# First batch of an attention and squared-ReLU kernel: another order of key scores, value sums and loads, zero products between the scores, and a shorter lag of the first output blocks

## The chip, the cores and the metric

The kernel runs on one core of a Trainium2 chip. The metric is the device time of one execution in microseconds (us), lower is better. TensorE is called PE, its weight loads PEld, VectorE DVE, ScalarE ACT, GpSimd POOL, and the queue that issues the transfers SP, as in the profile.

## The reference

Four batches of 12,480 tokens with 128 channels go through an attention with 49 agents, and the result through a two-layer network with 2,048 hidden units:

```python
def sm(a, b):
    s = (a @ b.transpose(0, 2, 1)) / np.sqrt(128)
    s = s - s.max(-1, keepdims=True)
    e = np.exp(s)
    return e / (e.sum(-1, keepdims=True) + 1e-09)
agent_v = sm(agents, k) @ v                  # 49 agents look at all keys of a batch
x = (sm(q, agents) @ agent_v).reshape(B * S, D)
h = x @ w_in                                 # 128 -> 2048
g = np.maximum(h, 0.0) ** 2
out = g @ w_out                              # 2048 -> 128
```

All of it is float32. The two weight matrices come as float64.

## The kernel before

*Pieces.* The 12,480 keys of a batch are cut into 13 pieces (`NS`) of 8 chunks (`G`) of 120 keys (`CH`). Queries are cut in the same way into groups of 960 tokens, 52 groups over the four batches. For a group the network runs in 16 blocks (`NF`) of 128 hidden units, so there are 832 blocks, counted by `i`.

*A block.* `mm1(i)` (L480) multiplies the group's attention weights, kept as a high and a low part, by `W`, the product of the batch's agent values and `w_in` (made by `w_make`, L356, L369, L371). `relu` (L484) and `square` (L488) run on ACT, `high` (L492) and `low` (L496) on DVE split the result in two parts, and `mm2` (L508) adds the block's product with `w_out` (as `wo_hi` and `wo_lo`) into two PSUM banks per group, in two halves of six matmuls. Between the halves of an `mm2` each bank changes the half of the rows that feeds it; an empty instruction on POOL's queue (`pass_on`, L161) takes the first half's end, and the second half waits for it (`take_over`). `mm2` of block i - `LAG` stands at place i, with `LAG` 6.

*The first batch.* Before any block can run, `W` of the first batch must be there, and for that all of its keys and values. Stage by stage: 12 products of zeros (`warm_up`, L652, 128x128 by 128x512, bf16); for each of 13 pieces a load, `k_scores` (L179: 8 float32 matmuls of a 128x120 key chunk as weights with the 49 agents, 16 records on PE), `k_copy` on ACT (L218) and `k_pmax` on DVE (L221); the maximum over pieces (`k_max`, steps 0 to 5, on DVE and PE). The maximum is taken twice: over the first 6 pieces (`S1`, into `mMs`), so that their exponentials can be taken early, and over all 13 (`mM`); `p_scale` corrects the sums of the first six. `k_sub` (L248) and `k_exp` (L251) follow per piece, then `v_acc_whole` (L298: 8 matmuls with 129 columns, 16 records) adds the piece's value sum into one of the two PSUM banks `vps` (pieces 0 to 5 into the first, 6 to 12 into the second). All 13 value sums come after all 13 key scores and the scores of the first query group (`q_scores`). Then `a_first` and `w_make` make `W`.

*Conversion.* `w_in` and `w_out` come in four pieces each as raw bits (`raw_load`). `to_f32` makes float32 of a piece in six steps, five on DVE (L85 to L90) and one on ACT (L86). `wo_split` makes `wo_hi` on ACT (L111) and `wo_lo` on POOL (L113). The last piece of `w_out` is converted during the first blocks.

*Order.* Nothing is left to a scheduler: `at(t, f, ...)` notes a step with a time, and the steps are issued in the order of these times; each engine works through its own list in this order and waits at semaphores. Steps of the first stage have times from `Z` = -100 on, the blocks have the time i. Extra work between the blocks (scores of later groups and of the next batch, `q_half`, `k_pair`) is placed by a planner (`chain`, with the sets `taken` and `banks`) or by hand for the first few: the pairs of key scores of batch 1 stand at 4.5 and 6.5.

*Buffers.* Loads of keys, values and queries rotate through 6 buffers (`io`), raw pieces through the 5 buffers that later hold `low` results (tag "gl"). SP issues loads in the order of the list `loads`, and waits with each until its buffer is free.

Of the kernel before, what the change touches and what calls it, by code (L numbers as in the profile page):

```python
# [17 lines left out]
P = 128  # L18
# [7 lines left out]
def agent_attention_relu2_kernel(ctx: ExitStack, tc: tile.TileContext, qT, kT, v, agT, w_in, w_out, outT):  # L26
# [10 lines left out]
    NF = F // P  # L37
    NS = NCH // G
# [29 lines left out]
    PW = 512  # L68
# [2 lines left out]

    raws = {}

    def raw_load(t, src):
        raws[t, src is wi_bits] = raw = ew.tile([P, PW, 2], U32, name="raw", tag="gl", bufs=5)
        nc.sync.dma_start(out=raw, in_=src[:, t * PW:(t + 1) * PW, :])

    def to_f32(raw, dst):

        lo, hi = raw[:, :, 0], raw[:, :, 1]  # L80
        p = ew.tile([P, PW], U32, name="cv_p", tag="g", bufs=3)
        x = ew.tile([P, PW], F32, name="cv_x", tag="gh", bufs=5)
        ts, stt = nc.vector.tensor_scalar, nc.vector.scalar_tensor_tensor
        return [
            lambda: ts(out=p, in0=hi, scalar1=20, scalar2=0x7FF, op0=ALU.logical_shift_right, op1=ALU.bitwise_and),  # L85
            lambda: nc.scalar.activation(p, p, AF.Relu, bias=ebias, scale=float(1 << 23)),  # L86
            lambda: ts(out=x.bitcast(U32), in0=hi, scalar1=0xFFFFF, scalar2=0x100000, op0=ALU.bitwise_and, op1=ALU.bitwise_or),
            lambda: stt(out=x, in0=lo, scalar=2.0 ** -32, in1=x.bitcast(U32), op0=ALU.mult, op1=ALU.add),
            lambda: stt(out=p, in0=hi, scalar=0x80000000, in1=p, op0=ALU.bitwise_and, op1=ALU.bitwise_or),
            lambda: stt(out=dst, in0=x, scalar=2.0 ** -20, in1=p.bitcast(F32), op0=ALU.mult, op1=ALU.mult),  # L90
        ]

    cv, wo = {}, {}
# [5 lines left out]

    def wo_make(t, step):  # L100
        if step == 0:
            wo[t] = ew.tile([P, PW], F32, name="wo_f", tag="gh", bufs=5)
            cv["o"] = to_f32(raws.pop((t, False)), wo[t])
        cv["o"][step]()

    def wo_split(t, step):
# [186 lines left out]
    S1 = 6  # L293
# [254 lines left out]
    def chain(t, todo):  # L548

        first = prev = None
        while todo:
            n = 1
            while todo[0][0] == "PE" and n < len(todo) and (todo[n][1] in reads_bank and todo[n][0] != "PE" or todo[n][1:-1] == todo[n - 1][1:-1] and todo[n][1] is not k_max):
                n += 1
            t += hop[prev][todo[0][0]] if prev else 0
            while True:
                g, p, ts = t, None, []
                for e, f, *_ in todo[:n]:  # L560
# [42 lines left out]
    def plan_turns(s):  # L603
        _, end = chain(max(ends[s] + 2, (s - 1) * NF), [("PE", q_transpose, s), ("ACT", q_copy, s)])
        at(end + .9, q_spread, s)
        assert end + 3 < s * NF, (s, end)
# [49 lines left out]
        early.close()  # L656
        ps_a[0] = ctx.enter_context(tc.tile_pool(name="ps_a", bufs=1, space=bass.MemoryType.PSUM))

    Z, KT, KP, VP = -100.0, 6.3, 1.7, 1.87
    FULL = (0, 1, 2, 3, 4, 5)  # L660
    loads = [(k_load, 0, n) for n in range(NS)]
    for x, *load in ((3, raw_load, 0, wi_bits), (6, raw_load, 1, wi_bits), (9, raw_load, 2, wi_bits), (13, raw_load, 3, wi_bits), (16, raw_load, 0, wo_bits)):
        loads.insert(x, load)
    loads += [(q_load, 0), *((v_load, 0, n) for n in range(NS)), (q_load, 1), *((k_load, 1, n) for n in range(AHEAD))]
    for x, t in ((22, 1), (26, 2), (30, 3)):
        loads.insert(x, (raw_load, t, wo_bits))
# [4 lines left out]
    def convert(f, n, times):  # L671
        for x, t in enumerate(times):
            at(Z + t, f, n, x)

    tk = [KT + KP * n + (.9 if n > S1 else 0) for n in range(NS + 1)]
    for n in range(NS):
        at(Z + tk[n], k_scores, 0, n)
        at(Z + tk[n] + KP + .01, k_copy, n)
        at(Z + tk[n] + KP + .05, k_pmax, n)
    for n in range(3):  # L680
        t = tk[n * 3 + (1 if n else 0)] + KP
        convert(win_make, n, (t + .6, t + .61, t + 1, t + KP + .7, t + KP + 1.3, t + 2 * KP + .7))
    t1, t2 = tk[S1], tk[NS] + 1.7
    for x, t in zip((0, 2, 3, 4, 5), (t1 + .7, t1 + 1.85, t1 + 2.3, t1 + KP + 2.3, t1 + KP + 2.8)):
        at(Z + t, k_max, x, S1, m2s[:, 0:1], mMs)
    for x, t in zip(FULL, (tk[NS] - 1.3, tk[NS] + .7, t2, t2 + .6, t2 + 2.4, t2 + 2.9)):
        at(Z + t, k_max, x)
    tv = [t2 + .5 + VP * n + (.5 if n else 0) + (1 if n > S1 + 2 else 0) for n in range(NS + 1)]
    for n in range(NS):
        at(Z + tv[n], v_acc_whole, n, vps)  # L690
        t = t1 + KP + 3 + .9 * n if n < S1 else t2 + 4 + 1.3 * (n - S1)
        at(Z + t, k_sub, n, nc.vector, mMs if n < S1 else mM)
        at(Z + t + .55, k_exp, n)
    for x, t in ((0, t2 + 3), (1, t2 + 3.1), (2, tv[S1] + .2), (3, tv[NS])):
        at(Z + t, p_scale, x, vps)
    t = tk[NS]
    for f, y in ((q_scores, 0), (q_max, 1.75), (q_sub, 2.4), (q_exp, 3), (q_total, 5.2), (q_norm, 6), (q_hi, 6.6), (q_lo, 7.2)):
        at(Z + t + y, f, 0, *([nc.vector] if f in (q_norm, q_lo) else []))
    at(Z + tv[S1 + 3] - 1, q_transpose, 0)
    at(Z + tv[S1 + 3] + .1, q_copy, 0)  # L700
    at(Z + tv[S1 + 3] + .2, q_spread, 0)
    for n in range(4):
        t = t2 + 7 + 3.8 * n
        convert(*((win_make, 3) if n == 0 else (wo_make, n - 1)), (t, t + .01, t + .4, t + 1.3, t + 2, t + 2.7))
        if n:
            at(Z + t + 3.4, wo_split, n - 1, 0)
            at(Z + t + 3.5, wo_split, n - 1, 1)
    t = tv[NS]
# [6 lines left out]
    for f in range(1, F // 512):  # L715
        for x, y in ((0, -.5), (2, -.49), (3, .06)):
            at(f + y, w_make, 0, f, x)
    convert(wo_make, 3, [-Z + .5 + .4 * x for x in range(6)])
    for x in range(2):
        at(3.5 + .1 * x, wo_split, 3, x)  # L720
    at(2.9, begin)
    at(3.5, q_half, 1, 0)
    at(4.02, q_half, 1, 1)
    at(4.03, q_shift, 1)
    _, ends[1] = chain(4, [("ACT", q_exp, 1), ("DVE", q_total, 1), ("DVE", q_norm, 1, nc.vector), ("ACT", q_hi, 1), ("DVE", q_lo, 1, nc.vector)])
    plan_turns(1)
    at(3.55, k_load, 1, AHEAD)
    for n, t in ((0, 4.5), (2, 6.5)):
        for x in range(2):
            at(t + .6 * x, k_pair, 1, n, x)  # L730
        at(t + 1, kp_copy, n, 2)
        at(t + 1.05, kp_max, n, 2)
    banks.update(range(10))
    taken.update((e, t) for e in ("ACT", "DVE") for t in (3, 4, 5, 6, 7, 8))
    plan_queries_early(2, 9, False)
    for s in range(3, NSG):
        plan_queries(s)
# [7 lines left out]
        ready = plan_values(b, ready, b * NS * NF)  # L745

    for i in range(NG + LAG):
        j, late = i - LAG, i < LAG or (i - LAG) % NF == 0
        if i < NG:
            at(i if late else i + .01, mm1, i)  # L750
            at(i + .1, relu, i)
            at(i + 1.2, square, i)
            at(i + 1.35, high, i)
            at(i + 3.3, low, i)
        if j >= 0:
            at(i + (.01 if late else 0), mm2, j, 0)
# [31 lines left out]
```

## Time and profile before

| what | value |
|---|---|
| runs of the kernel | 1990.84 to 1992.5 us, median 1991.76 (3 runs) |
| profiled execution | 1987.69 us, span 1985.9 us |
| busy: PE, PEld | 1970.5 us (99%), 1902.2 us (96%) |
| busy: DVE, ACT, POOL | 1777.6 us (90%), 1748.1 us (88%), 119.4 us (6%) |
| granted TensorE clock, mean over the span | 0.989 |
| moved by DMA | 121.31 MB, 61 GB/s in the mean |

The span goes from the first to the last instruction of the profiled execution, and the execution's own time is 1.8 us longer; this execution was 4.1 us shorter than the median of the runs. "Granted clock" is the share of full speed at which TensorE was allowed to run. In the profile's views a line stands for one or more instructions of the same kind, with the tiles written and read (`out<-in`), their number, and times in us; a bracket or a "<-" names what ended an engine's idle time. Lines are those of the kernel listed above.

### The profile page before, as it was taken

What the parts mean: (1) busy time and instruction counts of PE and PEld (TensorE: products, weight loads), DVE (VectorE), ACT (ScalarE), POOL (GpSimd) and SP (SyncE); (2) the same over time, 40 slices, a digit from 0 to 9 for tenths busy, and PEclk for the clock granted to TensorE, in tenths of its full rate; (3) what the DMA queues carried; (4) which work ended last, traced back from release to release, by engine and by line L of the source; (5) the groups of instructions that cost most, each with busy time, mean ns of one, the idle gap of its engine ahead of it and who ended that gap; (6) DMA issues with size and microseconds to landing.
All of it is one profiled execution on the core that took longest, in us unless ns stands there. A gap on an engine that the chain in (4) does not pass through costs nothing.

```text
span 1985.9 us, 47810 instructions
## 1 busy us (share of the span) xinstructions
PE 1970.5 (99%) x19919; PEld 1902.2 (96%) x19920; DVE 1777.6 (90%) x2434; ACT 1748.1 (88%) x2118; POOL 119.4 (6%) x56
## 2 busy tenths in 40 slices
PE   9999999999999999999999999999999999999998
PEld 8799999999998999999999899999999999999997
DVE  4677999999989999999998999999998998989887
ACT  2577998998889898998998999999999999999997
POOL 0100010000000040110000030020000000000000
PEclk6899999999999999999999999999999999999999
DMA  8431122122102112112111111121110101010000
GB/s 290 139 108 56 36 81 95 66 70 96 35 29 76 57 59 86 56 49 97 46 39 56 35 53 64 40 76 36 56 39 29 45 25 49 25 48 25 33 21 21
DMA packets 37434, 121.31 MB, mean 61 GB/s; under 512 B 4216, under 2 KB 9696, under 8 KB 37216
## 3 DMA queue, kind: packets, MB, share of 16 engines
q1 hardware_dynamic: 37216, 118.25, 17.5%
q8 instruction: 156, 2.56, 0.5%
q14 instruction: 62, 0.51, 0.1%
HBM read 82.89 MB, written 25.56 MB: 55 GB/s over the span
## 4 chain that ended last, share of the span: by engine, by line
PE 96%; ACT 2%; DVE 1%; issue 1%; POOLq 0%; ACTq 0%
PE out L508 54%; PE h L480 27%; PE ps_att L190 7%; PE ps_att L449 2%; PE ps_att L278 2%; PE out L298 1%; PE h L179 1%; ACT r L484 1%; ACT g L488 1%; PE ps_one L179 1%; DVE gl L496 1%; PE ps_att L362 0%; DVE gh L492 0%; PE out L652 0%; ACT w_a L369 0%
## 5 line engine op out<-in xcount | busy, mean ns | idle before, releaser
L484 ACT ACTIVATE r<-h 128x960 f32<-128x960 f32 x832 | 811.8, 976 | 167.3 <-PE h L480 141.7
L496 DVE TENSOR_TENSOR gl<-g,gh 128x960 fp32r<-128x960 f32 x832 | 958.6, 1152 | 0.0
L488 ACT ACTIVATE g<-r 128x960 f32<-128x960 f32 x832 | 834.5, 1003 | 2.2 <-DVE gl L496 1.3
L508 PE MATMUL out<-gh,wo_hi 64*128 64x480 f32 x3328 | 823.0, 388 | 5.5 <-POOLq L161 3.4
L508 PE MATMUL out<-gh,wo_lo 64*128 64x480 f32 x3328 | 804.3, 377 | 0.0
L508 PE MATMUL out<-gl,wo_hi 64*128 64x480 f32 x3328 | 803.0, 377 | 0.0
L492 DVE CAST gh<-g 128x960 fp32r<-128x960 f32 x832 | 558.8, 672 | 152.5 <-ACT g L488 98.7
L508 PEld LDWEIGHTS out<-gh,wo_hi 64*128 64x128 f32 x3328 | 471.8, 184 | 21.4 <-POOLq L161 9.6
L508 PEld LDWEIGHTS out<-gh,wo_lo 64*128 64x128 f32 x3328 | 476.7, 186 | 7.6
L508 PEld LDWEIGHTS out<-gl,wo_hi 64*128 64x128 f32 x3328 | 474.4, 185 | 9.7
L480 PE MATMUL h<-p_a,w_a 49*128 49x480 f32 x1664 | 410.7, 388 | 1.7 <-ACT r L484 1.1
L480 PE MATMUL h<-p_a,w_b 49*128 49x480 f32 x1664 | 402.0, 377 | 0.0
L480 PE MATMUL h<-p_b,w_a 49*128 49x480 f32 x1664 | 401.1, 376 | 0.0
L480 PEld LDWEIGHTS h<-p_a,w_a 49*128 49x128 f32 x1664 | 236.0, 184 | 10.0 <-ACT r L484 2.9
L480 PEld LDWEIGHTS h<-p_a,w_b 49*128 49x128 f32 x1664 | 237.3, 185 | 7.6 <-DVE w_b L371 0.4
L480 PEld LDWEIGHTS h<-p_b,w_a 49*128 49x128 f32 x1664 | 238.6, 187 | 4.9
L248 POOL TENSOR_TENSOR sk<-sk,mM 120x392 f32<-120x392 f32 x39 | 111.5, 2859 | 1230.7 <-PE out L508 645.3
L190 PEld LDWEIGHTS ps_att<-ag_sb,qt 64*120 64x120 f32 x1632 | 114.4, 181 | 1.2
L190 PE MATMUL ps_att<-ag_sb,qt 64*120 64x49 f32 x1632 | 106.5, 257 | 0.0
L190 PEld LDWEIGHTS ps_att<-ag_sb,kt 64*120 64x120 f32 x1248 | 79.3, 189 | 2.7 <-issue 1.8
L190 PE MATMUL ps_att<-ag_sb,kt 64*120 64x49 f32 x1248 | 76.0, 268 | 1.7 <-issue 1.7
L449 PEld LDWEIGHTS ps_att<-ident_r,pp 64*113 64x113 f32 (+1 forms) x816 | 55.0, 175 | 1.0 <-DVE pm L212 0.3
(126 smaller groups left out, 997.5 us busy)
## 6 DMA issues: line engine op xcount, KB each, us to landing
vt<-v SPq DMA_DIRECT2D x52, 516.0 KB
kt<-kT SPq DMA_DIRECT2D x52, 480.0 KB
qt<-qT SPq DMA_DIRECT2D x52, 480.0 KB
outT<-ob SPq DMA_DIRECT2D x51, 480.0 KB
p_b<-p_a SPq DMA_DIRECT2D x104, 91.9 KB
raw<-w_in SPq DMA_DIRECT2D x4, 512.0 KB
raw<-w_out SPq DMA_DIRECT2D x4, 512.0 KB
outT<-ob SPq DMA_DIRECT2D x2, 240.0 KB
```

What stands on the lines that cost most here:

```text
L179: nc.tensor.matmul(ps[:CH, c * A:(c + 1) * A], kt[:, c, :], ag_sb[:, b, :], start=True, stop=True)
L190: mm = nc.tensor.matmul(ps[:CH, u, r * A:(r + 1) * A], cols[u][r][rows], ag_sb[rows, b, :], start=x == 0 and r == 0, stop=x == 1 and r == ...
L248: eng.tensor_tensor(out=piece(n), in0=piece(n), in1=m.rearrange("p (o a) -> p o a", o=1).to_broadcast([CH, G, A]), op=ALU.subtract)
L278: nc.tensor.matmul(ps[:A2, t, :VW], pe[rows, c, :], vs[rows, c], start=c == 0, stop=c == G - 1)
L298: nc.tensor.matmul(ps[x][:A, :C + 1], piece(n)[:, c, :], vt[:CH, c, :], start=n in (0, S1) and c == 0, stop=c == G - 1 and n in (S1 - 1, N ...
L449: nc.tensor.matmul(ps[:M, t, c * n:(c + 1) * n], pps[s % 2][rows, c, :], ident_r[rows, rows], start=True, stop=True)
L480: nc.tensor.matmul(hs[i][:, t, :TT], w, p, start=n == 0, stop=n == 2)
L484: nc.scalar.activation(rs_[i], hs.pop(i)[:, :, :TT], AF.Relu)
L488: nc.scalar.activation(gs[i], rs_.pop(i), AF.Square)
L492: nc.vector.tensor_copy(ghs[i], gs[i])
L496: nc.vector.tensor_tensor(out=gls[i], in0=gs.pop(i), in1=ghs[i].bitcast(F32), op=ALU.subtract)
L508: mm = nc.tensor.matmul(o[u][:, :TT], w[rows, j, :], g[rows, u, :], start=j == 0 and x == 0 and n == 0, stop=j == NF - 1 and x == 1 and n ...
```

## The change

Seven things are changed, all of them in the first batch's stage and the first 20 blocks:

1. TensorE's order is written as one queue. Key scores of pieces 0 to 8 come first, with products of zeros between them (one after pieces 0 and 1, two after pieces 2 to 8: 16 in all, into the second `vps` bank, which holds nothing yet). Then value sums 0 to 3 alternate with key scores 9 to 12; then the query scores, the last maximum's two products with value sum 4 between them, and value sums 5 to 12.
2. The loads stand in that order, values among the keys.
3. `k_sub` and `k_exp` stand ahead of the value sum that needs them.
4. The seven conversions that lie before the blocks get times of their own. The last piece of `w_out` is loaded into an `io` buffer, converted at places 7.6 to 10.1 (before 0.5 to 2.5) in other buffers, and split at 11.5 (before 3.5).
5. `mm2` lags four blocks up to place 7, five up to place 13, and six after; at places 7 and 13 (`SKIP`) there is no `mm2`, and a pair of key scores of batch 1 stands there in its place.
6. `low` stands at i + 2.32 up to block 7 (before i + 3.3).
7. The first score half of query group 1 goes to 3.08 (before 3.5), the second to 4.005 (before 4.02); the planner may place other scores only from place 15 on (before 10).

```diff
+    SKIP = (7, 13)
...
+    queue = []
+    for n in range(S1 + 3):
+        queue += [("k", n, 1.7), ("w", 1 if n < 2 else 2, .22 if n < 2 else .44)]
+        if n in (S1, S1 + 1):
+            queue.append(("s", 2 * (n - S1 + 1), .45))
+    for n in range(S1 + 3, NS):
+        queue += [("v", n - S1 - 3, 1.87), ("k", n, 1.7)]
+    queue += [("q", 0, 1.7), ("m", 2, .45), ("v", S1 - 2, 1.87), ("m", 4, .45)]
+    for n in range(S1 - 1, NS):
+        queue.append(("v", n, 1.87))
+        if n == S1 + 2:
+            queue.append(("t", 0, 1.0))
+    for what, n, d in queue:
+        order[what, n] = t
...
+        at(Z + t, f, *args)
+        t += d
...
-    loads = [(k_load, 0, n) for n in range(NS)]
+    loads = [(k_load, 0, n) for n in range(S1 + 3)]
+    for n in range(S1 + 3, NS):
+        loads += [(v_load, 0, n - S1 - 3), (k_load, 0, n)]
+    loads += [(q_load, 0), *((v_load, 0, n) for n in range(NS - S1 - 3, NS)), (q_load, 1), *((k_load, 1, n) for n in range(AHEAD))]
+    for x, t, src in ((2, 0, wi_bits), (5, 1, wi_bits), (8, 2, wi_bits), (13, 3, wi_bits), (16, 0, wo_bits), (23, 1, wo_bits), (27, 2, wo_bits), (37, 3, wo_bits)):
+        loads.insert(x, (raw_load, t, src, x > 35))
...
-        t = t1 + KP + 3 + .9 * n if n < S1 else t2 + 4 + 1.3 * (n - S1)
+        t = t1 if n == 0 else max(t1 + .6 * n, order["v", n - 1] - .5) if n < S1 else t2 if n == S1 else order["v", n - 2] + .6
         at(Z + t, k_sub, n, nc.vector, mMs if n < S1 else mM)
         at(Z + t + .55, k_exp, n)
...
-    convert(wo_make, 3, [-Z + .5 + .4 * x for x in range(6)])
+    convert(wo_make, 3, [-Z + 7.6 + .5 * x for x in range(6)])
     for x in range(2):
-        at(3.5 + .1 * x, wo_split, 3, x)
+        at(11.5 + .1 * x, wo_split, 3, x)
...
-    for n, t in ((0, 4.5), (2, 6.5)):
+    for n, t in ((0, SKIP[0]), (2, SKIP[1])):
         for x in range(2):
-            at(t + .6 * x, k_pair, 1, n, x)
+            at(t - .005 + .025 * x, k_pair, 1, n, x)
...
     for i in range(NG + LAG):
-        j, late = i - LAG, i < LAG or (i - LAG) % NF == 0
+        lag = LAG - sum(i <= x for x in SKIP)
+        j, late = i - lag, i < lag or i in SKIP or (i - lag) % NF == 0
+        if i in SKIP:
+            j = -1
         if i < NG:
...
-            at(i + 3.3, low, i)
+            at(i + (2.32 if i <= SKIP[0] else 3.3), low, i)
```

More of the change, by code (lines that the diff above doesn't have):

```diff
@@ L72, in agent_attention_relu2_kernel, with raw_load, to_f32 @@
     raws = {}
-    def raw_load(t, src):
-        raws[t, src is wi_bits] = raw = ew.tile([P, PW, 2], U32, name="raw", tag="gl", bufs=5)
+    def raw_load(t, src, late=False):
+        raws[t, src is wi_bits] = raw = (io if late else ew).tile([P, PW, 2], U32, name="raw", tag="io" if late else "gl", bufs=None if late else 5)
         nc.sync.dma_start(out=raw, in_=src[:, t * PW:(t + 1) * PW, :])
-    def to_f32(raw, dst):
+    def to_f32(raw, dst, late=False):
         lo, hi = raw[:, :, 0], raw[:, :, 1]
-        p = ew.tile([P, PW], U32, name="cv_p", tag="g", bufs=3)
-        x = ew.tile([P, PW], F32, name="cv_x", tag="gh", bufs=5)
+        pool, tags = (wk, ("pe", "pe")) if late else (ew, ("g", "gh"))
+        p = pool.tile([P, PW], U32, name="cv_p", tag=tags[0], bufs=3)
+        x = pool.tile([P, PW], F32, name="cv_x", tag=tags[1], bufs=3 if late else 5)
         ts, stt = nc.vector.tensor_scalar, nc.vector.scalar_tensor_tensor
@@ L101, in wo_make @@
         if step == 0:
-            wo[t] = ew.tile([P, PW], F32, name="wo_f", tag="gh", bufs=5)
-            cv["o"] = to_f32(raws.pop((t, False)), wo[t])
+            late = t > 2
+            wo[t] = (io if late else ew).tile([P, PW], F32, name="wo_f", tag="io" if late else "gh", bufs=None if late else 5)
+            cv["o"] = to_f32(raws.pop((t, False)), wo[t], late)
         cv["o"][step]()
@@ L657, in begin @@
         ps_a[0] = ctx.enter_context(tc.tile_pool(name="ps_a", bufs=1, space=bass.MemoryType.PSUM))
-    Z, KT, KP, VP = -100.0, 6.3, 1.7, 1.87
-    FULL = (0, 1, 2, 3, 4, 5)
-    loads = [(k_load, 0, n) for n in range(NS)]
[L662 to L666, printed above, removed]
+    Z = -100.0
+    order, t = {}, 6.3
+    queue = []
[12 more added lines that the diff above has]
+        order[what, n] = t
+        f, args = {"k": (k_scores, (0, n)), "w": (warm_up, (n, 1)), "s": (k_max, (n, S1, m2s[:, 0:1], mMs)), "m": (k_max, (n,)),
+                   "v": (v_acc_whole, (n, vps)), "q": (q_scores, (0,)), "t": (q_transpose, (0,))}[what]
+        at(Z + t, f, *args)
+        t += d
+    last = t
+    assert all(order["v", n] > order["k", n] for n in range(NS))
+    loads = [(k_load, 0, n) for n in range(S1 + 3)]
[4 more added lines that the diff above has]
+        loads.insert(x, (raw_load, t, src, x > 35))
     for n, (f, *args) in enumerate(loads):
@@ L673, in convert @@
             at(Z + t, f, n, x)
-    tk = [KT + KP * n + (.9 if n > S1 else 0) for n in range(NS + 1)]
     for n in range(NS):
[L677 to L684, printed above, removed]
+        t = order["k", n] + 1.7
@@ L685, in agent_attention_relu2_kernel @@
+        at(Z + t + .01, k_copy, n)
+        at(Z + t + .05, k_pmax, n)
+    for x, t in ((0, order["k", S1 - 1] + 2.4), (3, order["s", 2] + .45), (5, order["s", 4] + .45)):
         at(Z + t, k_max, x, S1, m2s[:, 0:1], mMs)
-    for x, t in zip(FULL, (tk[NS] - 1.3, tk[NS] + .7, t2, t2 + .6, t2 + 2.4, t2 + 2.9)):
+    for x, t in ((0, order["k", NS - 1] + .7), (1, order["k", NS - 1] + 2.4), (3, order["m", 2] + .45), (5, order["m", 4] + .45)):
         at(Z + t, k_max, x)
-    tv = [t2 + .5 + VP * n + (.5 if n else 0) + (1 if n > S1 + 2 else 0) for n in range(NS + 1)]
+    t1, t2 = order["s", 4] + .7, order["m", 4] + .7
@@ L689, in agent_attention_relu2_kernel @@
     for n in range(NS):
-        at(Z + tv[n], v_acc_whole, n, vps)
-        t = t1 + KP + 3 + .9 * n if n < S1 else t2 + 4 + 1.3 * (n - S1)
+        t = t1 if n == 0 else max(t1 + .6 * n, order["v", n - 1] - .5) if n < S1 else t2 if n == S1 else order["v", n - 2] + .6
         at(Z + t, k_sub, n, nc.vector, mMs if n < S1 else mM)
         at(Z + t + .55, k_exp, n)
-    for x, t in ((0, t2 + 3), (1, t2 + 3.1), (2, tv[S1] + .2), (3, tv[NS])):
+    for x, t in ((0, t2 + .6), (1, t2 + .7), (2, order["v", S1 + 1]), (3, last)):
@@ L695, in agent_attention_relu2_kernel @@
         at(Z + t, p_scale, x, vps)
-    t = tk[NS]
-    for f, y in ((q_scores, 0), (q_max, 1.75), (q_sub, 2.4), (q_exp, 3), (q_total, 5.2), (q_norm, 6), (q_hi, 6.6), (q_lo, 7.2)):
+    t = order["q", 0] + 1.7
+    for f, y in ((q_max, .05), (q_sub, .7), (q_exp, 1.2), (q_total, 5.2), (q_norm, 6), (q_hi, 6.6), (q_lo, 7.2)):
         at(Z + t + y, f, 0, *([nc.vector] if f in (q_norm, q_lo) else []))
-    at(Z + tv[S1 + 3] - 1, q_transpose, 0)
-    at(Z + tv[S1 + 3] + .1, q_copy, 0)
-    at(Z + tv[S1 + 3] + .2, q_spread, 0)
@@ L702, in agent_attention_relu2_kernel @@
[L702 to L708, printed above, removed]
+    t = order["t", 0] + 1
+    at(Z + t, q_copy, 0)
+    at(Z + t + .1, q_spread, 0)
+    gap = 3.6
+    for n in range(7):
+        t = (9, 15, 27, 31.2, 35, 46, 52)[n]
+        d = 1.6 if n < 2 else 1
+        convert(*((win_make, n) if n < 4 else (wo_make, n - 4)), (t, t + .01, t + .4, t + 1 * d, t + 2 * d, t + 3 * d))
+        if n > 3:
+            at(Z + t + 3.6, wo_split, n - 4, 0)
+            at(Z + t + 3.7, wo_split, n - 4, 1)
@@ L709, in agent_attention_relu2_kernel @@
+    t = last
     at(Z + t + .1, warm_up, 3, 0)
@@ L717, in agent_attention_relu2_kernel @@
             at(f + y, w_make, 0, f, x)
-    convert(wo_make, 3, [-Z + .5 + .4 * x for x in range(6)])
+    convert(wo_make, 3, [-Z + 7.6 + .5 * x for x in range(6)])
     for x in range(2):
-        at(3.5 + .1 * x, wo_split, 3, x)
[L721 to L724, printed above, removed]
+        at(11.5 + .1 * x, wo_split, 3, x)
+    at(3.07, begin)
+    at(3.08, q_half, 1, 0)
+    at(4.005, q_half, 1, 1)
+    at(4.04, q_shift, 1)
+    banks.update([*range(5), *(x + y for x in SKIP for y in range(3))])
     _, ends[1] = chain(4, [("ACT", q_exp, 1), ("DVE", q_total, 1), ("DVE", q_norm, 1, nc.vector), ("ACT", q_hi, 1), ("DVE", q_lo, 1, nc.vector)])
+    taken.update((e, t) for e in ("ACT", "DVE") for x in SKIP for t in (x, x + 1))
     plan_turns(1)
     at(3.55, k_load, 1, AHEAD)
-    for n, t in ((0, 4.5), (2, 6.5)):
+    for n, t in ((0, SKIP[0]), (2, SKIP[1])):
         for x in range(2):
-            at(t + .6 * x, k_pair, 1, n, x)
[L731 to L734, printed above, removed]
+            at(t - .005 + .025 * x, k_pair, 1, n, x)
+        at(t + .5, kp_copy, n, 2)
+        at(t + .55, kp_max, n, 2)
+    banks.update(range(SKIP[1] + 2))
     plan_queries_early(2, 9, False)
```

## The prediction

> **What bounds the kernel now.** I read the page first (busy shares, then the 40 slices), then the core cut into windows at the moments where the granted clock changes, then the chain that ended last, the waits of PE, and the groups of instructions by shape up to 130 us.
>
> ```profile
> PE 1970.5 (99%) x19919; PEld 1902.2 (96%) x19920; DVE 1777.6 (90%) x2434; ACT 1748.1 (88%) x2118; POOL 119.4 (6%) x56
> ...
> PEclk6899999999999999999999999999999999999999
> ```
>
> TensorE is busy 99% of the span, so only what shortens TensorE's own work, or raises its clock, can move the end. The clock is short of full in the first two slices alone, which is where the whole change lies. The windows show where (columns: span, then busy time and count of each engine, granted clock, DMA share, GB/s):
>
> ```profile
> 6.77:10.18 3.41, 3.41 (x35) 3.41 (x34) 1.04 (x3) 0.50 (x2) 0.00 (x0) 1.00 0.98 310
> 10.18:13.59 3.41, 3.41 (x35) 3.41 (x35) 2.59 (x6) 1.76 (x4) 0.00 (x0) 1.00 1.03 420
> 13.59:17.01 3.42, 3.38 (x33) 3.29 (x32) 2.26 (x5) 1.26 (x3) 0.00 (x0) 1.00 1.02 416
> 17.01:44.31 27.30, 27.30 (x137) 26.88 (x136) 15.11 (x30) 7.50 (x16) 0.00 (x0) 0.50 0.75 268
> 44.31:47.73 3.42, 3.42 (x17) 2.88 (x16) 0.27 (x3) 0.53 (x1) 0.00 (x0) 0.50 0.81 297
> 47.73:70.06 22.33, 22.33 (x209) 21.92 (x208) 18.03 (x35) 9.35 (x18) 4.85 (x3) 1.00 0.86 278
> ...
> 78.45:81.86 3.41, 2.89 (x19) 1.54 (x18) 2.24 (x4) 3.41 (x6) 0.00 (x0) 1.00 0.00 0
> 81.86:85.27 3.41, 2.54 (x40) 2.20 (x36) 3.41 (x6) 3.30 (x5) 0.39 (x1) 1.00 0.01 2
> 85.27:95.51 10.24, 8.85 (x76) 8.66 (x78) 6.01 (x12) 4.50 (x6) 1.35 (x1) 0.50 0.01 2
> 95.51:98.93 3.42, 3.31 (x20) 2.34 (x20) 2.43 (x3) 2.28 (x3) 0.00 (x0) 0.50 0.00 0
> ```
>
> The clock is halved twice: from 17.01 to 47.73 (30.72 us) and from 85.27 to 98.93 (13.66 us). Half of that, 15.4 and 6.8 us, is lost. The full stretch before the first fall is 10.24 us; 10.24, 30.72 and 13.66 are 3, 9 and 4 times 3.41, so the clock is judged every 3.41 us. In the three windows before the first fall PE is busy without a gap, so it is not idle time that lowers it. The chain (start, length, what) shows what the array streams there:
>
> ```profile
> 1.22 5.30 PE out L652 x12
> 6.52 1.80 PE h L179 x16
> ...
> 13.36 1.68 PE h L179 x16
> ...
> 33.55 3.20 PE ps_one L179 x16
> ...
> 46.95 0.56 PE ps_one L243 x2
> 47.52 14.42 PE out L298 x128
> 61.94 0.91 PE h L449 x10
> 62.85 7.22 PE out L298 x64
> ...
> 71.39 1.20 PE out L652 x5
> 72.59 1.09 PE ps_one L356 x2
> ...
> 113.25 0.66 PE out L508 x6
> ```
>
> A value-sum record takes 7.22/64 = 113 ns for 129 columns, 0.87 ns a column. A key-score record has 49 columns, worth 43 ns of streaming, and takes 1.68/16 = 105 ns: the weight load sets its time (PEld 3.41 of 3.41). So key scores stream 41% of the time, and value sums 100%. Under 41% the clock fell after three windows (the third, with a gap, has 39%). Before the second fall I add up, from the same rows, three w_make records and six pairs of block matmuls of 0.22 us (about 64%), then four such pairs and two score halves (about 40%). The clock rose after 44.31:47.73, which holds 2.6 us of value sums (about 82%).
>
> **The change, part by part.** All times are against the profiled execution, 1987.69 us with a span of 1985.9; the runs have a median of 1991.76, so I subtract the gain from that.
>
> *Key scores to value sums.* The new order on TensorE, at full clock from the first key score at 6.52: 13 key and 1 query scores at 1.68 (23.5), 0.1 for the slower first one (1.80), 13 value sums at 1.805 (23.5), four small max products, 0.2 and 0.28 twice (1.0), the transposes (0.9). Added are 16 zero products: one after each of k0 and k1, two after each of k2 to k8. Twelve took 5.30 at half clock, so 0.22 each at full clock; five took 1.20, so 0.24. The next weight load hides behind the first of each group, so less than 0.22 is possible; I take 0.2, 3.2 in all, between 2.8 and 3.8. Sum 52.2: the last value sum ends at 58.7 in place of 70.06, **-11.4**.
>
> Does another engine or a load break this row?
>
> ```profile
> L251 ACT ACTIVATE sk<-sk 120x392 f32<-120x392 f32 x13 | 6.6, 524 | 3.4 <-DVE sk L248 3.4
> L221 DVE TENSOR_REDUCE pm<-h 120x49 f32<-120x392 f32 x8 | 4.5, 567 | 14.4 <-ACT sk L218 14.4
> ...
> L88 DVE SCALAR_TENSOR_TENSOR cv_x<-raw,cv_x 128x512 f32<-128x512 uint32 x8 | 5.5, 689 | 0.1
> ...
> L248 DVE TENSOR_TENSOR sk<-sk,mM 120x392 f32<-120x392 f32 x7 | 3.9, 559 | 0.0
> L218 ACT COPY sk<-h 120x392 f32<-120x392 f32 x8 | 3.9, 486 | 17.5 <-PE h L179 17.5
> ...
> L85 DVE TENSOR_SCALAR cv_p<-raw 128x512 uint32<-128x512 uint32 x8 | 3.4, 422 | 0.3 <-DMA raw<-w_in 0.3
> ...
> L225 DVE TENSOR_REDUCE m<-pm 120x49 f32<-120x294 f32 x1 | 0.7, 653 | 0.0
> ```
>
> First maximum: after k5 come copy 0.49, piece maximum 0.57, reduction 0.65, 1.7 in all, under k6 and four zero products (2.5). Its broadcast, then copy 0.2, subtraction 0.56 and exponential 0.52, lies under k8 and two (2.1). The last maximum: 0.49, 0.57, 0.2 after k12 lies under the query scores (1.68); 1.3 after its broadcast lies under v5 (1.8). These are covered, the last two by about 0.4 each; if DVE runs that late, v6 is late by the rest. DVE has 13 maxima, 13 subtractions and seven conversions of two steps of 0.42 and three of 0.69, 2.9: with the small steps some 38 us in 52, with the conversions put between. Loads: the five windows to 44.31 moved 268 to 420 GB/s; by 17.01 that is 3.9 MB from 6.77 on, and the agents and k0, 0.6 MB, were in before, since k0 was being scored: 4.5. k5, due at 16.5, ends the first 4.1 MB of the new queue (six key tiles of 480 KB, two raw pieces of 512 KB, the agents). A pair of tiles afterwards is 1.0 MB in 3.5 us, 290 GB/s, which 47.73:70.06 nearly shows. So I cost the new load order at nothing; if it fails, one tile late is 1.2 us.
>
> *The ramp.* Four blocks run before the first output product, where there were six; the pairs of key scores move to places 7 and 13, where no output product stands. The work is the same, so only idle time and clock count.
>
> ```profile
> PE ps_att L190 <- issue: 1.7, 1, 1.7
> ...
> PE h L480 <- ACT r L484: 1.1, 2, 0.5
> PE h L480 <- ACT w_a L369: 0.7, 1, 0.7
> ```
>
> Before: 3.5 us of idle PE plus 6.8 of clock, 10.3 lost. After: the 0.7 stays; the two waits for relu stay, since ACT's work up to block 4 is the same (1.3 with the second a little longer); the 1.7 goes, as the pair of key scores no longer waits for the bank that the query scores of group 1 hold. What is late next is ACT:
>
> ```profile
> L484 ACT ACTIVATE r<-h 128x960 f32<-128x960 f32 x19 | 18.5, 975 | 12.9 <-PE h L480 12.7
> L488 ACT ACTIVATE g<-r 128x960 f32<-128x960 f32 x18 | 18.0, 1001 | 0.1
> ...
> L86 ACT ACTIVATE cv_p<-cv_p,ebias 128x512 uint32<-128x512 uint32 x8 | 5.8, 722 | 5.9 <-DVE cv_p L85 5.9
> ...
> L111 ACT CAST wo_hi<-wo_f 128x512 fp32r<-128x512 f32 x4 | 2.5, 615 | 5.6 <-DVE wo_f L90 5.6
> ...
> L369 ACT CAST w_a<-h 113x512 fp32r<-113x512 f32 x2 | 1.2, 595 | 0.1
> ```
>
> Issue to issue these steps take ACT some 0.1 less than they last, 0.87 and 0.89 a block. To relu 10 that is 18.5, with four w_a (1.9), one conversion step (0.6), the exponential and hi part of group 1 (0.9) and the copy of the key pair (0.7), 22.6; PE needs 20.1 for what it does until then. Blocks 10 to 12 therefore wait about 1.0. Then the split of the last quarter of w_out, moved to place 11.5: its POOL step waits for ACT's wo_hi, and the relay of output block 7 (line 161) stands behind it on POOL. Such a relay behind a waiting POOL step costs PE time at three places later, one of them here:
>
> ```profile
> 215.25 0.49 PE L508 MATMUL out<-gh,wo_hi 64*128 64x480 f32 x2 [0.80 <-POOLq L161]
> ...
> PE out L508 <- POOLq L161: 3.4, 3, 1.6
> ```
>
> ACT reaches wo_hi about 2.2 after PE wants the relay; bounds are 0 (ACT has caught up) and 4 (the POOL step itself, 1.7, counts too). I take 2.2. Sum after: 0.7 + 1.3 + 0.1 + 1.0 + 2.2 = 5.3, so **-5.0**, bounds -2 and -8. Should the clock fall once here, PE is dense with output products and gets it back after one window, 1.7. The rest (conversions in other buffers, "low" a block earlier for blocks 0 to 7) moves off PE and costs nothing while PE is 99% busy; it has ACT at 88% and DVE at 90% to cover it.
>
> Total -16.4: 1991.76 - 16.4 = **1975.4**, if the clock holds through the key scores.
>
> **Does it hold?** A key score and two zero products: 16 x 43 + 2 x 213 ns of streaming in about 2.06 us, 54%; with one product 49%. What fell: single windows of 39% and 40%; what stood: 41%, 64% and more. By single windows the new share is clear of the limit. By pairs of windows what fell is 40% and about 52%, what stood about 66%: there 54% lies just over the higher one, near a coin toss. I take "holds" because no counting puts it under a share that fell, at a chance of 0.54.
>
> **Rivals.**
> *The zeros do not hold it (0.28).* It falls at 17.01 as before. The 8.2 us of work left to the end of k8 take 16.5, to 33.5; v0 takes 3.6 at half clock, fills a window at over 82% and lifts the clock by 37.5 to 40.9. Then 31.4: the last value sum ends at 68.8 to 70.4, against 70.06. The zeros eat what the overlap brings: -1.3 at best, with the ramp -6.3, **1985.5**. For it: the pair count. Against it: 41% stood twice. [...]
>
> *Slower (0.07).* The clock falls at 17.01, and in the mixed stretch every window has half a value sum and half a key score, (100 + 41)/2 = 70%, below the 82% that lifted it. A pair takes 7.0 at half clock, two windows 6.8, so the split hardly drifts. Then v0 to k12 stay cold and the last value sum ends near 80.0: +9.9 - 5.0, **1996.7**. It decides where the limit to rise is over 70% and the phase is bad.
>
> *Nothing measurable (0.11).* The clock falls a window or two earlier (10.18: the last value sum near 75.6, +5.5) and the ramp's -5.0 pays for it: **1992**. One value sum in the mixed stretch that waits for DVE would be 0.5 to 1 and is inside the ranges.
>
> **How the numbers follow.** Holds: 1975.4, its own range 1972 to 1980. The range for 8 in 10 takes in the second case: 1972 to 1988. Within 0.2% (4 us, what a measurement here can tell) are the last rival and a little of the first. Faster 0.82, same 0.11, slower 0.07.
>
> **What would show it.** Granted clock 1.00 from about 6.8 to the first output product; the last value sum near 59; no wait of PE before q_half of group 1; PE waiting for line 161 once near the 12th block, 1 to 3 us. Wrong if the clock reads 0.50 anywhere between 17 and 40, or if value sums of the mixed stretch wait for ACT or a load.

## The result, and the profile after

| | before | after |
|---|---|---|
| median of the runs, us | 1991.3 (1990.84 to 1992.5) | 1980.05 (1978.1 to 1980.49) |
| ratio, 95% interval | | 0.9941 (0.9923 to 0.9958) |
| profiled execution, span, us | 1987.69, 1985.9 | 1980.49, 1978.7 |
| mean granted clock | 0.989 | 0.996 |

The change gains 11.25 us by the medians, and 7.2 by the two profiled executions, since that of before ran some 4 us under its median. One run of an experiment (one zero, 2405.95 us at a granted clock of 0.744) is left out of the times below. In the changed kernel the lines quoted here stand two or three higher: L298 is L300, L179 is L181, L190 is L192, L480 is L482, L508 is L510, L161 is L163, L652 is L655.

The page's first part and its row of the clock, in 40 slices:

```profile
PE 1962.1 (99%) x19932; PEld 1880.4 (95%) x19936; DVE 1778.7 (90%) x2434; ACT 1748.2 (88%) x2118; POOL 108.3 (5%) x56
...
PEclk9989999999999999999999999999999999999999
```

TensorE executes more (the zeros) and is busy 8.4 us less: at a granted clock of 0.50 the work took about twice as long (in the chain of before a key score takes 3.20 us where it takes 1.68 at 1.00). The first slices now read 9; the third reads 8, so something fell there that had not fallen before. The windows cut at the clock's changes (span, busy time and count of each engine, granted clock, DMA share, GB/s):

```profile
6.90:99.07 92.17, 87.89 (x804) 75.40 (x807) 67.38 (x120) 49.85 (x77) 6.33 (x4) 1.00 0.63 223
92.24:95.65 3.41, 2.46 (x24) 1.78 (x20) 3.38 (x6) 3.41 (x6) 0.00 (x0) 1.00 0.00 0
95.65:99.07 3.42, 2.43 (x40) 2.33 (x40) 3.29 (x4) 2.64 (x4) 1.29 (x1) 1.00 0.73 226
99.07:109.31 10.24, 10.24 (x72) 9.00 (x70) 5.38 (x7) 4.54 (x5) 0.00 (x0) 0.50 0.25 89
109.31:130.00 20.69, 20.69 (x224) 19.20 (x224) 17.34 (x25) 17.20 (x21) 0.00 (x0) 1.00 0.06 25
1085.52:1088.93 3.41, 1.78 (x16) 1.28 (x15) 3.41 (x6) 3.20 (x4) 0.71 (x1) 1.00 0.00 0
1088.93:1092.35 3.42, 3.42 (x22) 2.81 (x20) 2.60 (x3) 0.53 (x1) 1.02 (x1) 0.50 0.00 0
```

From 6.90 to 99.07 the clock is full: the fall at 17.01 is gone. It falls at 99.07 for 10.24 us (5.1 lost) and at 1088.93 for 3.42 (1.7 lost). Before, 44.4 us were at half clock, in 42.9 of which PE was busy, so 21.4 were lost; now it is 13.7, all busy, and 6.8 lost. The chain that ended last and, below it, two answers of the timeline (start, length, what; a bracket gives the idle time ahead and what ended it):

```profile
14.10 0.43 PE out L655 x2
14.53 1.62 PE h L181 x16
...
25.41 1.90 PE out L300 x16
27.32 1.81 PE ps_one L181 x16
...
96.57 0.03 POOLq L163
...
96.64 0.92 PE out L510 x5
97.56 1.62 PE ps_att L192 x24
99.18 1.32 PE h L482 x5
```

```profile
56.83 2.82 PE L300 MATMUL out<-vt,sk 120*49 120x129 f32 x24
...
96.61 1.29 POOL L115 TENSOR_TENSOR wo_lo<-wo_f,wo_hi 128x512 fp32r<-128x512 f32 x1 [38.66 <-ACT wo_hi L113]
...
100.30 3.28 PE L192 MATMUL ps_att<-ag_sb,kt 64*120 64x49 f32 x32
103.36 0.75 PE L510 MATMUL out<-gh,wo_hi 64*128 64x480 f32 x2
```

The last value sum ends at 59.65 (before 70.06). At place 12 PE waits for the relay L163, which stands on POOL behind the split of `w_out`; the relay is let go at 96.57, as that split begins. The wait of PE, here and in the whole span:

```profile
PE out L510 <- POOLq L163: 1.9, 1, 1.9
PE out L510 <- POOLq L163: 5.2, 4, 1.9
```

It spreads over two windows (3.41 - 2.46 and 3.42 - 2.43, 0.95 and 0.99), the second of which also holds the first half of the moved pair of key scores (L192); at its end the clock falls.

### The profile page after: what moved, and what is told of

Its sections match the earlier page's. It is cut to its first block, busy times and chain, and to the rows that moved or that the text cites. A ratio compares the mean times of both kernels' runs of the same rounds, so it can differ in the third digit from the quotient of the medians.

```text
span 1978.7 us, 47839 instructions
## 1 busy us (share of the span) xinstructions
PE 1962.1 (99%) x19932; PEld 1880.4 (95%) x19936; DVE 1778.7 (90%) x2434; ACT 1748.2 (88%) x2118; POOL 108.3 (5%) x56
## 4 chain that ended last, share of the span: by engine, by line
PE 93%; ACT 3%; DVE 2%; issue 1%; DMA 0%; SPq 0%; POOLq 0%; ACTq 0%; DVEq 0%
PE out L510 53%; PE h L482 26%; PE ps_att L192 7%; PE ps_att L451 2%; PE ps_att L280 2%; ACT r L486 1%; PE out L300 1%; ACT g L490 1%; PE h L181 1%; DVE gh L494 1%; DVE gl L498 1%; PE ps_att L364 0%; PE out L655 0%; PE ps_one L181 0%; DMA p_b<-p_a 0%
## 5 line engine op out<-in xcount | busy, mean ns | idle before, releaser
L510 PE MATMUL out<-gh,wo_hi 64*128 64x480 f32 x3328 | 817.3, 389 | 7.9 <-POOLq L163 5.2
L510 PE MATMUL out<-gh,wo_lo 64*128 64x480 f32 x3328 | 798.4, 378 | 0.0
L510 PE MATMUL out<-gl,wo_hi 64*128 64x480 f32 x3328 | 797.3, 377 | 0.0
L510 PEld LDWEIGHTS out<-gh,wo_hi 64*128 64x128 f32 x3328 | 467.2, 185 | 26.1 <-POOLq L163 11.5
L510 PEld LDWEIGHTS out<-gl,wo_hi 64*128 64x128 f32 x3328 | 469.3, 185 | 12.4
L510 PEld LDWEIGHTS out<-gh,wo_lo 64*128 64x128 f32 x3328 | 471.3, 187 | 10.0
L482 PE MATMUL h<-p_a,w_a 49*128 49x480 f32 x1664 | 407.6, 389 | 1.6 <-ACT w_a L371 0.7
L482 PE MATMUL h<-p_b,w_a 49*128 49x480 f32 x1664 | 398.6, 377 | 0.3 <-DMA p_b<-p_a 0.3
L482 PE MATMUL h<-p_a,w_b 49*128 49x480 f32 x1664 | 398.7, 377 | 0.0
L482 PEld LDWEIGHTS h<-p_a,w_a 49*128 49x128 f32 x1664 | 233.4, 185 | 10.9 <-ACT r L486 2.1
L482 PEld LDWEIGHTS h<-p_b,w_a 49*128 49x128 f32 x1664 | 236.2, 188 | 7.2 <-DMA p_b<-p_a 0.8
L482 PEld LDWEIGHTS h<-p_a,w_b 49*128 49x128 f32 x1664 | 234.6, 186 | 7.9
L250 POOL TENSOR_TENSOR sk<-sk,mM 120x392 f32<-120x392 f32 x39 | 100.7, 2582 | 1223.2 <-PE out L510 696.9
L192 PEld LDWEIGHTS ps_att<-ag_sb,qt 64*120 64x120 f32 x1632 | 114.3, 181 | 1.6
L192 PE MATMUL ps_att<-ag_sb,qt 64*120 64x49 f32 x1632 | 106.3, 258 | 0.0
L192 PEld LDWEIGHTS ps_att<-ag_sb,kt 64*120 64x120 f32 x1248 | 77.7, 185 | 0.7
L192 PE MATMUL ps_att<-ag_sb,kt 64*120 64x49 f32 x1248 | 74.3, 264 | 0.0
```

Source lines behind the costliest of these rows:

```text
L192: mm = nc.tensor.matmul(ps[:CH, u, r * A:(r + 1) * A], cols[u][r][rows], ag_sb[rows, b, :], start=x == 0 and r == 0, stop=x == 1 and r == ...
L250: eng.tensor_tensor(out=piece(n), in0=piece(n), in1=m.rearrange("p (o a) -> p o a", o=1).to_broadcast([CH, G, A]), op=ALU.subtract)
L482: nc.tensor.matmul(hs[i][:, t, :TT], w, p, start=n == 0, stop=n == 2)
L510: mm = nc.tensor.matmul(o[u][:, :TT], w[rows, j, :], g[rows, u, :], start=j == 0 and x == 0 and n == 0, stop=j == NF - 1 and x == 1 and n ...
```

## The experiments

The theory: the zeros hold the clock through the key scores, by what streams in one window; what is lost in the ramp is one stall behind the relay and the fall that follows it. The rivals: the new order does it without the zeros; the fall in the ramp comes from the pair of key scores, whatever the relay does.

**The relay freed.** The POOL step of the last split goes three places later; nothing else changes.

```diff
-        at(11.5 + .1 * x, wo_split, 3, x)
+        at(11.5 + 3 * x, wo_split, 3, x)
```

> The changed kernel with one step moved: the POOL half of the last w_out split goes from place 11.6 to 14.5, behind the relays of output blocks 7 and 8; ACT's half stays at 11.5. Theory (the relay held on POOL stops PE for 1.9 us, and this gap brings the fall of the clock that follows for 10.24 us): both go, 1.9 + 5.1 = 7 us less than the change, about 1973; no 0.50 clock after 60 us in the first 130. Rival A (the clock falls there anyway, because ACT feeds too few output products in the ramp): only the 1.9 goes, about 1978. Rival B (PE would have waited for ACT at the next block anyway): no difference, 1980.

Measured 1971.13 us (1970.95 to 1973.09), ratio 0.9903 (0.9877 to 0.9928); the span is 1971.3 against 1978.7 of the changed kernel. Its windows at the same place:

```profile
92.24:95.65 3.41, 3.41 (x48) 3.17 (x44) 3.23 (x6) 3.41 (x6) 0.00 (x0) 1.00 0.08 24
95.65:99.07 3.42, 3.42 (x58) 3.31 (x58) 2.87 (x4) 3.39 (x5) 0.00 (x0) 1.00 0.84 270
99.07:109.31 10.24, 10.24 (x114) 9.21 (x112) 9.53 (x11) 8.66 (x10) 1.30 (x1) 1.00 0.22 68
```

No gap, no fall, with the pair of key scores in its place: 114 PE records in the last stretch instead of 72. The stall was the cause. It had cost 1.9 by itself and 5.1 by the clock. The profiled spans differ by 7.4 and the medians by 8.9, where 7 was forecast.

**No zeros.** The changed kernel without its 16 zero products.

```diff
-        queue += [("k", n, 1.7), ("w", 1 if n < 2 else 2, .22 if n < 2 else .44)]
+        queue += [("k", n, 1.7)]
```

> The changed kernel without the 16 zero products between the key scores; all else, the mixing of value sums and key scores too, stays. Theory (the zeros hold the clock): it falls near 17 us, the first value sum lifts it again at 31 to 34, and the last value sum ends at 63 to 66 in place of 59.6: 4 to 6 us slower than the change, 1984 to 1986. Rival (the mixing holds the clock, the zeros only cost): the clock stays at 1.00 and 16 x 0.2 = 3.3 us are saved, 1977.

Measured 1987.81 us (1982.07 to 1996.52), ratio 0.9989 (0.997 to 1.0008). Its windows:

```profile
7.12:17.36 10.24, 10.04 (x96) 9.95 (x95) 5.96 (x12) 3.69 (x8) 0.00 (x0) 1.00 1.02 406
17.36:31.01 13.65, 13.65 (x68) 12.89 (x66) 6.44 (x13) 2.85 (x7) 0.00 (x0) 0.50 0.86 329
```

The fall is back after three windows, but lasts four and not nine, because value sums now start at 27.5; the last one ends at 63.9. So the new order shortens the fall and the zeros prevent it. The loss against the changed kernel is 4.0 by the profiled spans, as forecast, and 7.8 by the medians, which is more than the forecast 4 to 6; the runs spread over 14 us.

**Zeros alone.** The kernel before, with 24 zeros put between its 13 key scores.

```diff
+        at(Z + tk[n] + 1, warm_up, 1 if n < 2 else 2, 1)
```

> The kernel before with zero products alone: one after each of the first two key scores and two after each of the other 11, 24 in all, nothing reordered. Theory (the clock is all that the new first stage earns; reordering does not shorten PE's own work): the clock stays at 1.00 until the value sums end near 60 (70.06 less 15.4 and plus 24 x 0.21 = 5.0), 10 us faster than before, 1981, with before's ramp and its own fall of the clock behind. Rival (zeros at half the stream share do not last over 13 key scores, the early value sums are needed): a fall between 17 and 40 costs 5 us or more, 1986 or above.

Measured 1984.34 us (1976.11 to 1985.77), ratio 0.9954 (0.9937 to 0.9971). Its windows and its last four value sums in the chain:

```profile
4.67:59.28 54.61, 54.61 (x485) 50.95 (x484) 39.15 (x78) 20.54 (x41) 4.84 (x3) 1.00 0.96 354
72.93:107.07 34.14, 32.72 (x244) 29.32 (x242) 16.04 (x22) 14.94 (x20) 1.74 (x1) 0.50 0.03 7
```

```profile
51.89 7.22 PE out L298 x64
```

The value sums end at 59.1, no later than in the changed kernel (59.65). Part of that is the earlier rise of the clock during the warm-up (4.67 against 6.90), which lets the first key score start at 5.67 and not at 6.52; counted from there it is 53.4 against 53.1. So in the first stage the zeros alone earn all but 0.3 us, and the new order and the new loads add this 0.3, with eight zeros fewer. The old ramp then gives most of it back: it falls for 34.1 us, where the kernel before fell for 13.7. The forecast was 1981. The runs are of two kinds, four at 1976.1 to 1979.7 (clock 0.995 to 0.997) and six at 1984.3 to 1985.8 (0.991 to 0.993); the profiled one is of the second kind, so the long fall in the ramp is shown for that kind alone.

**The new first stage with the old ramp.**

```diff
-    SKIP = (7, 13)
+    SKIP = ()
...
-    convert(wo_make, 3, [-Z + 7.6 + .5 * x for x in range(6)])
+    convert(wo_make, 3, [-Z + .5 + .4 * x for x in range(6)])
...
-    for n, t in ((0, SKIP[0]), (2, SKIP[1])):
+    for n, t in ((0, 4.5), (2, 6.5)):
...
```

> The changed kernel's first stage with the ramp of before: output products six blocks behind from the start, pairs of key scores at 4.5 and 6.5, the last w_out piece converted at 0.5 and split at 3.5. Theory (the first stage earns about 10.4 us, and the new ramp nothing on balance, since its relay stall and the clock's fall give back what it saves): as the change, 1979 to 1982. Rival (the new ramp earns its 5 us and the first stage less): 1985.

Measured 1982.31 us (1976.18 to 1987.67), ratio 0.9955 (0.994 to 0.9971). Value sums end at 59.4; then:

```profile
74.64:95.12 20.48, 17.86 (x136) 16.19 (x138) 11.26 (x16) 6.71 (x10) 0.82 (x1) 0.50 0.09 25
```

2.6 us of gaps are lost there, and half of the 17.9 busy us to the clock, 8.9. The median lies 0.3 over the forecast 1979 to 1982. The new ramp as it was changed is worth about 2 by the medians (1982.3 against 1980.05; the ratios' intervals overlap), and with the relay freed 11 (1971.1, the same first stage).

**The new ramp alone.** The kernel before with the new ramp, relay freed.

```diff
+    SKIP = (7, 13)
...
-        at(3.5 + .1 * x, wo_split, 3, x)
+        at(11.5 + 3 * x, wo_split, 3, x)
...
-    for n, t in ((0, 4.5), (2, 6.5)):
+    for n, t in ((0, SKIP[0]), (2, SKIP[1])):
...
+        lag = LAG - sum(i <= x for x in SKIP)
...
```

> The first stage of the kernel before, without zeros and in its old order, with the new ramp (four blocks behind at first, pairs of key scores at 7 and 13, the last w_out piece late in other buffers) and the POOL half of its split at 14.5 as in relay_free. Theory (ramp and first stage add up: the ramp of before loses 10.3 us to idle time and the clock, the new one without the held relay about 2.3): 8 us faster than before, 1984, with the clock's fall at 17 us left and none after the value sums. Rival (the new ramp gains only behind a first stage that holds the clock): within 3 us of before.

Measured 1985.18 us (1983.72 to 1987.43), ratio 0.9978 (0.9969 to 0.9988): 4.4 gained, a miss by almost half. In its profile the clock falls already at 12.20 and stays low until 49.75, 37.6 us where it was 30.7 before, so the value sums end at 72.8 and not at 70.06. That is 2.8 of the 3.3 us by which block 0's relu starts later than before. From there to block 420 this ramp gains 5.8, and it has no fall. Why the clock falls 4.8 us earlier, with the same key scores, can be read in the chain at the fourth key score:

```profile
3.08 7.99 DMA kt<-kT
11.07 0.04 issue
11.11 2.48 PE ps_one L181 x16
```

PE pauses there for the fourth piece of keys, which lands at 11.07. The window from 8.79 to 12.20 holds this pause, and by my count (explained below) it streams 35%; the first three windows of the kernel before stream 39, 39 and 37, and there the fall came after the third.

**One zero, and twice as many.** From the relay freed: one product after every key score (9), or two and four (32).

```diff
-        queue += [("k", n, 1.7), ("w", 1 if n < 2 else 2, .22 if n < 2 else .44)]
+        queue += [("k", n, 1.7), ("w", 1, .22 if n < 2 else .44)]
```

```diff
-        queue += [("k", n, 1.7), ("w", 1 if n < 2 else 2, .22 if n < 2 else .44)]
+        queue += [("k", n, 1.7), ("w", 2 if n < 2 else 4, .22 if n < 2 else .44)]
```

> The kernel of relay_free with one zero product after each of the nine key scores in place of two after seven of them: seven fewer. Streaming share there falls from about 54% to 49%. Theory (anything clearly over the 39 to 41% under which the clock fell will do): the clock holds, 7 x 0.21 = 1.5 us less than relay_free's 1971.1, 1969.6. Rival (the limit lies between 49% and 54%, the second zero is needed): a fall between 14 and 24 us, the last value sum at 63 to 68 in place of 59.6, 1975 to 1980.

> The kernel of relay_free with twice the zero products (32 in place of 16), the order of all other steps unchanged: the price of a zero product by itself. Theory (the clock holds with either, a zero costs PE its own 0.21 us): 16 x 0.21 = 3.4 us more than relay_free, 1974.5. Rival A (part of them hides behind waits of PE for copies and loads): under 2 us more, 1973 or less. Rival B (two were not always enough, so that relay_free falls in some runs): faster than relay_free.

One zero: 1973.13 us, ratio 0.9934 (0.9911 to 0.9958). The runs are of two kinds: six lie at 1969.6 to 1973.4 with a mean clock of 0.998 or more, three at 1984.0 to 1986.9 with 0.991 to 0.992. The profiled one, at 1969.6, is what was forecast and has no fall. So one zero is the cheaper cure when the clock holds. Where it fell in those three runs is not shown, since none of them was profiled; a run with two zeros was like them once (the last experiment, 1988.41). Twice as many: 1977.22 us (1976.47 to 1977.7), ratio 0.9935 (0.9919 to 0.9951). The end of the value sums, in its chain and in that of the relay freed:

```profile
55.95 7.22 PE out L300 x64
```

```profile
52.42 7.22 PE out L300 x64
```

3.53 for 16 more zeros, 0.22 each: nothing of a zero hides. The spans differ by 3.7, near the forecast 3.4; the medians, taken at different times, by 6.1.

**Narrow zeros.** From the relay freed: each product of 512 columns becomes four of 16 columns, with the same weights.

```diff
+    def narrow(n, t):
+        for _ in range(4 * n):
+            nc.tensor.matmul(vps[t][:, :16], warm[:, :P], warm[:, :16], start=True, stop=True)
...
-        f, args = {"k": (k_scores, (0, n)), "w": (warm_up, (n, 1)), "s": (k_max, (n, S1, m2s[:, 0:1], mMs)), "m": (k_max, (n,)),
+        f, args = {"k": (k_scores, (0, n)), "w": (narrow, (n, 1)), "s": (k_max, (n, S1, m2s[:, 0:1], mMs)), "m": (k_max, (n,)),
```

> The kernel of relay_free with each of the 16 zero products of 512 columns replaced by four of 16 columns with the same 128 columns of weights: about as many instructions and weight loads more, but almost nothing streamed. Theory (the clock is held by the columns that stream through the array): the share stays at about 40%, the clock falls between 14 and 21 us and is back with the first value sums; 10 us or more over relay_free's 1971, 1981 to 1990. Rival (any matmuls between the key scores, a break in their pattern or more instructions, hold it): the clock stays at 1.00, within 3 us of relay_free.

Measured 1983.37 us (1979.23 to 2000.47), ratio 0.998 (0.9954 to 1.0007). Its windows:

```profile
6.77:10.18 3.41, 3.41 (x41) 3.41 (x40) 1.24 (x3) 0.86 (x2) 0.00 (x0) 1.00 0.99 365
10.18:37.49 27.31, 27.31 (x184) 27.07 (x184) 12.29 (x25) 6.53 (x13) 0.00 (x0) 0.50 0.76 275
```

In the first window PE and its weight loads are busy all the time, and the clock falls at its end. More instructions did not hold it here: between the same times PE has 41 records, and 33 in the relay freed, whose clock stays at 1.00 through the key scores. The wide zeros, which stream more columns, did.

**The second stall.** From the relay freed: `k_sub` of the next batch goes on POOL two places later. In the relay freed PE still waits three times for a relay, longest from 1079.23 to 1080.86, where the relay stands on POOL behind a `k_sub` that waits for the maximum.

```profile
PE out L510 <- POOLq L163: 3.3, 3, 1.6
```

```diff
-            chain(max(t0, t - 4), [("POOL", k_sub, n)])
+            chain(max(t0 + 2, t - 4), [("POOL", k_sub, n)])
```

> The kernel of relay_free with the subtractions of the later batches on POOL placed two blocks later (from the end of the maximum + 2 on), so that the first of each batch does not wait on POOL for the maximum with the relays behind it. Theory (a waiting POOL step holds the relays and PE): the gaps of 0.84, 0.81 and 1.63 us near 219, 613 and 1080 us go, and with the last the fall of the clock at 1082 for 3.41 us: 3.3 + 1.7 = 5.0 less, 1966. Rival (PE would wait there for something else, or the exponentials come late and the later steps slide): within 1 us of relay_free.

Measured 1967.23 us, ratio 0.9899 (0.9874 to 0.9924); all runs but one lie between 1966.86 and 1970.27, that one at 1988.41 with a clock of 0.988. The span is 1965.5 at a mean clock of 1.000, against 1971.3 and 0.999 of the relay freed, and no wait for the relay is left in its trace. The spans differ by 5.8 and the medians by 3.9, where 5.0 was forecast. The ratios of the two overlap, so it is the traces that separate them. It is the fastest version here.

## Why the prediction was right, and where it was off

*The clock holds.* Right, and for the reason named: the zeros hold it (no zeros falls at 17.36, the changed kernel not before 99.07), and the streamed share counts (narrow zeros fall at 10.18). For key scores these traces settle the doubt between single windows and pairs. I count streamed columns from the records of all these traces. The price of a column is my estimate: two zeros of 512 columns take 0.43 us, so 0.42 ns for a column of zeros or of a block matmul, and twice that, 0.83, for a column of the float32 scores and value sums (a value sum's record took 0.87); two matmuls side by side in the two halves of the rows count half each (in before, from 215.57 on, two of 480 columns start every 0.22 us). What the prediction called 41, 41 and 39% is 39.3, 38.8 and 37.1 so, and the window before the second fall, about 40% there, is 34. Among key scores the clock fell after windows of 34.8, 35.0, 37.1 and 37.8% (one each in before, no zeros, the new ramp alone and narrow zeros) and stood after 38.6% and more; and pairs of 39 to 47% stood, below the 48.5 (the prediction's 52) that the pair count needs to have fallen. Most of these windows come from later runs, so the prediction could not have settled it.

*The first stage, -11.4.* Measured -10.4. A key score after zeros takes 1.62 and two zeros 0.43, 2.05 together, as forecast. But a value sum next to a key score takes 1.90 and the key score 1.81, where 1.805 and 1.68 were taken from rows in which each kind followed itself: 0.2 a pair, four pairs. The covers held: no wait of PE for an exponential or a load is in the chain.

*The first stage's cause.* The gain was put to zeros and order together; zeros alone give all but 0.3 of it. The order is a second cure for the same fall (63.9 without zeros), and the two don't add.

*The ramp, -5.0.* This step failed: in the profiled executions the lead over the kernel before shrinks behind the value sums, from 10.4 to 7.2. The stall at place 12 came where it was forecast and was sized well, 1.9 against 2.2. The clock behind it was mis-sized and left out of the sum: "PE is dense with output products and gets it back after one window, 1.7". It took three windows, 5.1. The pair of key scores that the change itself moved to place 13 stands right behind the stall: from 100.30 to 103.58 PE streams 41%, and by my count the three windows hold 60, 79 and 100%. The clock rose after the third. The prediction had the window after which it rose in the kernel before (82%) and the place of the pair, and did not lay one on the other. How long the fall would have been with the stall and without the pair was not run.

Three smaller terms were off as well. "Blocks 10 to 12 therefore wait about 1.0" for ACT: no such wait is in the trace. The 10.3 us lost before were counted too high: 1.5 us of the idle time lie in the windows at half clock (10.24 - 8.85 and 3.42 - 3.31) and stand in the sum a second time by half. And "the work is the same" does not quite hold. I took PE's busy time from the end of the value sums to the relu of block 831, less half of what ran at half clock: 1886.6 to 1887.3 us in the eight profiles with the new ramp, 1884.7 to 1885.6 in the three with the old one, with the same number of matmuls. Why the same matmuls take longer there stays open.

*A stall far from the change.* The fall after 1088.93, 1.7, lies in work of the next batch; a 1.63 us wait for the relay fell within one window. The kernel before has the same wait (1.64, up to 1096.92), but there the edge of two windows cuts it, 0.34 and 1.30, and the clock stood. So this fall came with the shift of the work against the windows. The prediction looked no further than the first 20 blocks.

*The sum.* Against the profiled execution it gave 1971.3, and 1980.49 came: 9.2 short. Of that the first stage is 1.0, the fall in the ramp 5.1, the late one 1.7, the longer busy time 1.3 and the idle time counted twice 0.7; idle time grew by 1.0 where 1.8 was forecast, which gives 0.8 back, and 0.2 is left. Taken from the median, the forecast is 4.65 off: 1980.05 lies inside the range of 1972 to 1988, at the edge of the 1972 to 1980 that was given for a clock that holds, so the time alone would not have told the two cases apart. Some of that closeness is luck: the profiled execution of before was 4 under its median, that of after at the top of its runs.

The lead over the kernel before, by the start of ACT's relu of four blocks, shows where it went (us):

| relu of block | changed | relay freed | zeros alone | old ramp | new ramp alone |
|---|---|---|---|---|---|
| 0 | -9.8 | -10.4 | -11.0 | -10.6 | +3.3 |
| 16 | -12.6 | -19.9 | | | |
| 420 | -8.6 | -16.0 | -1.9 | -6.7 | -2.5 |
| 831 | -7.2 | -14.6 | -2.0 | -6.7 | -2.7 |

At block 16 some scores of later groups are still put off, so the lead there is partly borrowed; by block 420 it is paid. The row of 420 for the relay freed, -16.0, looks like the prediction's sum of -16.4, but that sum held 2.2 for the stall, which is gone there. Like for like it is -18.6 against -16.0.

## What to carry to other kernels

In this case the granted clock fell to 0.50 although TensorE never stopped: in narrow zeros PE and its weight loads were busy 3.41 of 3.41 us from 6.77 to 10.18, and the clock fell at 10.18. Wide products that need nothing, between the same key scores, kept it at 1.00 (from 6.90 to 99.07 in the changed kernel). So where matmuls wait for their weight loads, count the streamed columns in each 3.41 us window, and try such products where they fall short. Behind a stall, look at what stands next on TensorE: with dense work next the fall took one window (97% streamed behind 1088.93, by my count), and with a pair of key scores next it took three (10.24 us from 99.07), so keep sparse work away from places that can stall. Look also at what stands ahead of an empty instruction on a lightly used queue: L163 waited on POOL behind the split of `w_out` until 96.57, and PE 1.9 us for it.

## What the hardware showed that was not expected

The clock fell after a single window (narrow zeros, full only from 6.77 to 10.18), and behind gaps of 1.6 and 1.9 us. The wait of 1.63 or 1.64 us for the relay in the next batch is in ten of the eleven profiles. Where an edge between windows cut it, the clock stood, four times of four (in one zero the edge cuts off only 0.03 us, and the window streams 46%); where it lay whole in one window, the clock fell five times of six. The sixth (the old ramp, near 1089) streams 41% in that window and the five 37 to 40, which would fit, but one window before a fall, behind the value sums of zeros alone, holds 42%, so between blocks the count does not separate the two. The windows after which the clock rose held 80.7% and more by the same count; it did not rise after one of 79.4%, nor after one of 81.4% (the old ramp). A relay on POOL was held by a wait ahead of it (PE waited 1.9 us at place 12) and, as the profile shows it, not by a running instruction: in the trace of before, two of L161's passed at 249.88 and 251.85 while a POOL `k_sub` shown from 247.09 for 5.55 us ran (a span on POOL is rough). And the spread among runs of one kernel follows its granted clock, about 2 us for a thousandth (narrow zeros: 1979.23 us at 0.994, 2000.47 at 0.983). Kernels that hardly fall in their profile mostly repeat closely (relay freed, 2 us from end to end; the last version, 3.4 without its one run at 1988.41), and those that fall often do not (no zeros, 14 us).
